# Layer-norm statistics straight from PSUM, shared work and a new instruction order in a fused gated-attention and MLP kernel

## The chip, the cores and the metric

The kernel runs on one core of one Trainium2 chip. The metric is the device time of one execution in microseconds (us).

## The reference

A gated linear attention with complex decay, then a layer norm with a two-layer MLP and a residual. B = 4 batches, H = 8 heads, S = 768 tokens, D = 48 per head, model width H x D = 384, hidden width 1536, all float32 at the outside.

```python
mag = np.sqrt(a_re * a_re + a_im * a_im)
scale = np.minimum(mag, 0.999) / (mag + 1e-06)
a_re_n, a_im_n = (a_re * scale, a_im * scale)
for t in range(S):                                   # state S_re + i S_im: D x D per head
    ar, ai = a_re_n[:, :, t, :, None], a_im_n[:, :, t, :, None]
    new_re = ar * S_re - ai * S_im
    new_im = ar * S_im + ai * S_re
    S_re, S_im = (new_re + np.einsum('bhd,bhe->bhde', k[:, :, t], v[:, :, t]), new_im)
    y[:, :, t] = np.einsum('bhd,bhde->bhe', q[:, :, t], S_re)
x = y.transpose(0, 2, 1, 3).reshape(B, S, H * D)
mu, var = mean(x), mean((x - mu) ** 2)
xn = (x - mu) / np.sqrt(var + 1e-06) * g_ln
out = x + np.maximum(xn @ w_ch1, 0.0) @ w_ch2
```

## The kernel before

The tokens are cut into 24 chunks of 128 (n = 0 to 23), worked in 12 pairs P of two chunks (`R = 2`); a batch is three pairs. Pair 0 does its front half in two parts of four heads (`PARTS`). For each pair:

- **Decay and phase.** `are`, `aim` are loaded; ScalarE (ACT) takes logs and exponentials (`ln`, `iv`, `u`), VectorE (DVE) or GpSimd the ratio `r`, its square `r2`, the log magnitude `l` and its clip `lc`. TensorE (PE) sums logs over tokens (`dec`) and angles (`ph`), ACT makes `e` and `en` (growth for queries, decay for keys), then `sin` and `cos` (`trig`). ACT's tables for logs and for trigonometry are switched by `tab`. In the pairs of `QUARTER` the cosine comes from a quarter turn added by PE (`qt`), in the others from an absolute value (`abs`).
- **Keys and queries.** `ke = k * en`, `qe = q * e`; `ks` and `qs` hold the product with the cosine (operation `.0`) and with the sine (`.1`) side by side. They are transposed by PE (`kT`, `qT`, copied to `ksT`, `qsT`) or, where the plan says S, by a DMA of the SP queue.
- **Attention.** `am` scores, `atm` masks them (DVE, or `ac` on ACT and a select on GpSimd), `y` sums values and the state `G` into a PSUM bank; `gm`, `G` carry the state, `dps` and `decc` its decay.
- **Norm.** `x` copies y from PSUM to SBUF as bf16, `bn` takes mean and variance of x, `xc` subtracts the mean, `xtr` transposes on PE and `xT` copies back. `rstd` is applied only at the end, to the MLP's output, as the ReLU lets it through.
- **MLP.** `ws` multiplies the 9 pieces of w_ch1 by g once. `mm1.P.g.part` (6 matmuls of 256 columns each) fills a group of four hidden tiles, `relu.P.g` writes them to `h`, `mm2.n.g` (4 matmuls of 384 columns) adds the group to the output bank. `ot` is `rstd * o + x`, in one DVE operation, or as `oa` on ACT and an addition on GpSimd; `st` stores it.

The weights are loaded by GpSimd's queue: `wl.0` to `wl.2` for w_ch1, `wl.3` to `wl.5` for w_ch2; all other loads, stores and DMA transposes stand in the SP queue.

Nothing is scheduled by a compiler. The order of all instructions is written out in the string `PLAN`: each token names an operation, its engine (P, A, V, G or S) and, behind it, the PSUM bank (8 in all); `@name` makes an operation of GpSimd or DVE wait for another one, so that they take turns at a port that they share. Each engine works its tokens strictly in this order. Tiles come from rings (`RINGS`), so a load waits until the tile of three pairs ago is read. `warm` operations are matmuls on constants that fill PE's waits at the start; 25 stand in the plan.

Of the kernel before, what the change touches and what calls it, by code (L numbers as in the profile page):

```python
# [41 lines left out]
qrow:G mask:G aim.1.0:S r.0.1:V one:G are.2.0:S pick:G@r.0.1 r2.0.1:A aim.2.0:S iv.0.0:A r.0.0:V r2.0.0:V
gln:S u.0.1:A ln.1.0:A k.0.1:S are.3.0:S l.0.1:V q.1.1:S lc.0.1:V u.0.0:A k.0.0:S warm.0:P0 warm.1:P0
warm.2:P0 warm.3:P0 warm.4:P0 warm.5:P0 warm.6:P0 warm.7:P0 warm.8:P0 dec.0.1:P6 l.0.0:V iv.1.0:A lc.0.0:V
zdec:V ln.2.0:A e.0.1:A6 iv.2.0:A r.1.0:V r2.1.0:V u.1.0:A r.2.0:V warm.9:P0 dec.0.0:P7 e.0.0:A7 l.1.0:V
en.0.0:A7 lc.1.0:V warm.10:P0 warm.11:P0 warm.12:P0 warm.13:P0 warm.14:P0 warm.15:P0 warm.16:P0 dec.1.0:P0
# [5 lines left out]
cos.0.1:A4 car.1.0:A2 ks.0.1.1:V ks.0.0.1:V qe.0.1.0:V qs.0.0.1:V ks.0.0.0:V ks.0.1.0:V qs.0.1.1:V qs.0.1.0:V
qs.0.0.0:V sin.1.0:A2 kT.0:P4 kT.1:P0 vf.1.0:S qT.0:P1 ksT.0:V4 ksT.1:V0 qt.1.0:P2 wl.2:G qT.1:P4 qsT.0:V1
warm.22:P5 am.0:P0 aim.3.0:S tab.log.2:A en.2.0:A6 e.2.0:A6 qsT.1:V4 v.0:G@qs.0.0.0 gm.0:P5 am.1:P6 ks.1.0.1:G
qe.1.0.0:G atm.0:V0 iv.3.0:A qs.1.0.1:G tab.trig.3:A cos.1.0:A2 q.2.0:S warm.23:P4 ph.2.0:P0 G.0:A5 y.0:P4
x.0:A4 atm.1:V6 warm.24:P6 y.1:P2 ws.1.0:V qs.1.0.0:V are.4.0:S ws.1.2:V ws.0.0:V sin.2.0:A0 bn.0:V gm.1:P5
x.1:A2 G.1:V5 ks.1.0.0:G@ws.0.0 bn.1:V xc.0:V qT.3:P4 qsT.3:A4 qt.2.0:P0 qT.2:P2 ws.0.1:V ws.0.2:A xc.1:V
kT.3:P6 cos.2.0:A0 aim.4.0:S v.1:G@xc.1 kT.2:P7 ksT.3:V6 xtr.1:P3 qsT.2:A2 xtr.0:P3 am.3:P0 ws.2.0:A xT.0:V3
ws.1.1:A ksT.2:V7 gm.2:P6 mm1.0.0.0:P4 q.3.0:S r.3.0:G am.2:P2 mm1.0.0.1:P4 qe.2.0.0:G atm.3:V0 atm.2:V2
q.2.1:S G.2:A6 y.3:P0 th.3.0:A r2.3.0:G gm.3:P6 ph.3.0:P2 x.3:A0 relu.0.0:V4 bn.3:V y.2:P7 tab.log.4:A  # L60
ln.4.0:A x.2:A7 mm1.0.1.1:P0 u.3.0:A k.2.0:S mm1.0.1.0:P0 ws.2.1:V wl.3:G ws.2.2:V mm1.0.2.0:P4 wl.4:G
# [5 lines left out]
en.3.0:A2 mm2.0.1:P6 mm2.1.1:P7 kT.4:P0 vf.2.1:S l.4.0:V lc.4.0:V kT.5:P5 rstd.0:G dec.4.0:P2 k.3.0:S
qe.3.0.1:G@lc.4.0 qsT.5:V1 ksT.4:A0 mm2.1.2:P7 ksT.5:V5 are.5.0:S k.3.1:S mm2.0.2:P6 am.4:P4 ot.1:V7
qe.3.0.0:G qs.3.0.0:V ph.4.0:P0 qs.3.0.1:V e.4.0:A2 qT.7:P7 en.4.0:A2 atm.4:V4 ke.3.0.0:G@qs.3.0.1 am.5:P2
v.2:A are.6.0:S aim.5.0:S ot.0:V6 ke.3.0.1:G car.4.0:A0 ln.5.0:A iv.5.0:A mm2.3.0:P4 y.4:P6 aim.6.0:S x.4:A6  # L70
qsT.7:V7 k.4.1:S mm2.2.0:P5 ks.3.0.0:V vf.3.1:S ln.6.0:A gm.4:P7 vf.3.0:S mm2.2.1:P5 qT.6:P6 G.4:A7 q.4.0:S
ks.3.0.1:V rstd.1:G atm.5:V2 q.4.1:S abs.4.0:A0 kT.6:P7 bn.4:V y.5:P2 mm2.2.2:P5 k.4.0:S r.5.0:G q.5.0:S
qsT.6:V6 k.5.0:S mm2.3.1:P4 ksT.6:V7 kT.7:P3 ot.2:V5 ksT.7:V3 iv.6.0:A am.6:P6 x.5:A2 mm2.3.2:P4 tab.trig.7:A
th.5.0:A r.6.0:G ac.6:A6 vf.4.0:S bn.5:V ph.5.0:P2 v.3:G xc.4:V xtr.4:P5 xc.5:V xtr.5:P5 k.6.0:S sin.4.0:A0
atm.6:G@xc.5 am.7:P6 qe.4.0.1:G st.1:S dps.3:P0 sin.5.0:A2 abs.5.0:A2 ke.4.0.0:G ot.3:V4 xT.4:V5 gm.6:P1
mm1.2.1.0:P4 decc.3:V0 G.6:A1 st.0:S vf.4.1:S are.7.0:S y.6:P0 x.6:A0 atm.7:V6 mm1.2.1.1:P4 ke.4.0.1:G gm.7:P1
qe.4.0.0:G bn.6:V y.7:P0 x.7:V0 bn.7:V mm1.2.2.0:P6 rstd.2:G xc.6:V r2.5.0:A relu.2.1:A4 aim.7.0:S
mm1.2.2.1:P6 xc.7:V cos.5.0:A th.6.0:A ks.4.0.1:V mm1.2.0.0:P4 xtr.6:P2 xtr.7:P2 are.8.0:S are.9.0:S xT.6:V2
dps.4:P0 decc.4:V0 G.7:V1 mm1.2.0.1:P4 mm1.3.2.1:P2 vf.5.0:S r2.6.0:G@ks.4.0.1 mm1.3.2.0:P2 mm1.3.0.0:P0
cos.4.0:A relu.2.0:V4 ks.4.0.0:G relu.2.2:V6 tab.log.8:A u.6.0:A v.4:V u.5.0:A l.5.0:V k.5.1:S mm1.3.0.1:P0  # L80
relu.3.0:A0 mm2.5.0:P4 mm1.3.1.1:P6 mm2.4.0:P5 qs.4.0.1:V relu.3.2:A2 qs.4.0.0:V ln.7.0:A iv.7.0:A mm2.5.1:P4
kT.9:P2 lc.5.0:V rstd.3:G dec.5.0:P0 en.5.0:A0 l.6.0:V lc.6.0:V ln.8.0:A mm2.4.1:P5 e.5.0:A0 qT.8:P3 ksT.9:V2
mm1.3.1.0:P6 ksT.8:S r.7.0:G@lc.6.0 mm2.4.2:P5 qsT.8:V3 dec.6.0:P2 ke.5.0.1:G qsT.9:S am.8:P0 iv.8.0:A
relu.3.1:V6 ke.5.0.0:V st.2:S ks.5.0.1:V ks.5.0.0:G@ks.5.0.1 gm.8:P6 mm2.5.2:P4 e.6.0:A2 en.6.0:A2 r2.7.0:A
u.7.0:A q.6.0:S atm.8:V0 mm2.6.0:P7 am.9:P2 vf.6.0:S G.8:A6 ot.5:V4 ph.6.0:P0 y.8:P4 car.6.0:A0 mm2.6.1:P7
gm.9:P6 x.8:A4 q.5.1:S tab.trig.9:A th.7.0:A q.6.1:S q.7.1:S atm.9:V2 qe.5.0.0:G y.9:P4 mm2.6.2:P7 ot.4:V5
bn.8:V mm2.7.0:P5 x.9:V4 kT.11:P4 vf.5.1:S qe.5.0.1:G abs.6.0:A0 qs.5.0.1:G bn.9:V l.7.0:V qs.5.0.0:V k.6.1:S
ph.7.0:P2 sin.6.0:A0 mm2.7.1:P5 qT.10:P0 st.3:S oa.6:A7 ksT.10:S xc.8:V xtr.8:P7 xc.9:V lc.7.0:V G.9:V6
aim.8.0:S car.7.0:A2 ke.6.0.1:G@lc.7.0 sin.7.0:A2 ke.6.0.0:G aim.10.0:S are.10.0:S xtr.9:P7 xT.8:V7 qT.11:P1
ksT.11:V4 mm2.7.2:P5 abs.7.0:A2 mm1.4.2.1:P2 qe.6.0.0:G ot.6:G mm1.4.2.0:P2 cos.6.0:A qsT.10:V0 qe.6.0.1:G  # L90
k.7.0:S tab.log.10:A ln.9.0:A qsT.11:V1 mm1.4.0.0:P6 st.4:S dps.6:P4 mm1.4.0.1:P6 v.5:G dec.7.0:P0 relu.4.2:V2
mm1.4.1.0:P2 decc.6:V4 rstd.4:G mm1.4.1.1:P2 qs.6.0.1:V relu.4.0:A6 mm2.8.0:P4 aim.9.0:S en.7.0:A0 qs.6.0.0:V
e.7.0:A0 am.11:P6 gm.10:P0 relu.4.1:A2 k.7.1:S ks.6.0.1:V q.7.0:S q.8.0:S mm2.9.0:P1 iv.9.0:A am.10:P2 r.8.0:V
mm2.8.1:P4 mm2.9.1:P1 atm.11:V6 G.10:V0 y.11:P0 atm.10:V2 vf.6.1:S qe.7.0.1:G@r.8.0 ks.6.0.0:G r.9.0:G y.10:P2
q.9.1:S ot.7:V5 mm2.9.2:P1 tab.trig.11:A cos.7.0:A th.8.0:A ph.8.0:P6 x.11:V0 kT.12:P5 x.10:A2 mm2.8.2:P4
bn.11:V bn.10:V v.6:G xc.11:V xtr.11:P0 th.9.0:A xc.10:V xtr.10:P0 qsT.12:S ot.9:V1 abs.8.0:A6
# [694 lines left out]
```

## Time and profile before

| | |
|---|---|
| runs (3) | 186.75, 186.89, 187.06 us; median 186.89 |
| profiled execution | 187.27 us, its span 185.6 us, granted clock 1.00 |
| busy | PE 173.0, ACT 160.4, DVE 153.7, GpSimd 103.6 us |
| moved by DMA | 37.29 MB, mean 201 GB/s |
| first matmul, last matmul's end | 2.2 us, 181.4 us |

The span is what the profile covers of an execution; the 1.67 us around it (187.27 - 185.6) are start and end. Busy times of engines overlap and don't add up to the span. PE is TensorE's matmuls, PEld its weight loads, DVE VectorE, ACT ScalarE, POOL GpSimd, SP the queue that issues most DMAs; L12 is line 12 of the kernel.

### The profile page before, as it was taken

How to read it: one execution, taken by the hardware profiler on the slowest of the kernel's cores; microseconds unless marked ns; L12 is line 12 of the kernel's file. 1: busy time of each engine (PE TensorE's matmuls, PEld its weight loads, DVE VectorE, ACT ScalarE, POOL GpSimd, SP SyncE). 2: the span in 40 equal slices, each digit the busy share in tenths (PEclk: the TensorE clock that was granted, in tenths of full speed). 3: DMA queues.
4: the chain of work that ended last, by engine and by line, in shares of the span. 5: the costliest groups of instructions: out<-in, count | busy, mean ns of one | idle time of the engine just before them, and what ended most of it. 6: DMA issues, size and time to landing. Idle time of an engine off the chain costs nothing.

```text
span 185.6 us, 4962 instructions
## 1 busy us (share of the span) xinstructions
PE 173.0 (93%) x1950; PEld 134.8 (73%) x1950; DVE 153.7 (83%) x298; ACT 160.4 (86%) x218; POOL 103.6 (56%) x120
## 2 busy tenths in 40 slices
PE   5887898899999999999999999999998999999990
PEld 4765576778677798777787787878776779787760
DVE  2578899999989889999889999999979987767222
ACT  5789999999999999999999999989999898536460
POOL 8203757877479699377779733374454528360110
PEclk9999999999999999999999999999999999999999
DMA  5999999899998999999999999999999999993222
GB/s 142 291 254 209 184 209 234 208 201 193 246 277 172 215 252 288 150 197 224 232 276 199 198 228 188 221 220 214 171 225 160 197 150 262 178 202 113 91 78 87
DMA packets 131879, 37.29 MB, mean 201 GB/s; under 512 B 126096, under 2 KB 131856, under 8 KB 131856
## 3 DMA queue, kind: packets, MB, share of 16 engines
q1 hardware_dynamic: 129072, 34.62, 90.0%
q0 software_dynamic: 2784, 2.36, 8.2%
q8 instruction: 15, 0.25, 0.5%
q14 instruction: 8, 0.07, 0.1%
HBM read 28.31 MB, written 4.72 MB: 178 GB/s over the span
## 4 chain that ended last, share of the span: by engine, by line
PE 74%; ACT 12%; DMA 5%; DVE 4%; issue 1%; SPq 1%; POOL 1%; POOLq 0%; ACTq 0%; DVEq 0%
PE banks L724 24%; PE banks L703 23%; PE banks L597 6%; DMA are<-in_a_re_dram 5%; PE banks L574 4%; PE banks L457 3%; ACT L759 3%; PE banks L476 2%; PE banks L647 2%; PE banks L675 2%; PE banks L650 2%; PE banks L625 2%; ACT w L428 1%; ACT th L465 1%; PE banks L472 1%
## 5 line engine op out<-in xcount | busy, mean ns | idle before, releaser
L724 PE MATMUL banks<-w2b,h 128*128 128x384 bf16 x288 | 54.9, 326 | 0.0
L703 PE MATMUL banks<-xT,w1b 128*128 128x256 bf16 x432 | 52.2, 272 | 0.2 <-DVE ksT L284 0.2
L703 PEld LDWEIGHTS <-w1b 128*128 128x128 bf16 x432 | 41.0, 98 | 6.2 <-issue 0.6
L724 PEld LDWEIGHTS <-h 128*128 128x128 bf16 x288 | 26.0, 97 | 13.3 <-ACT h L714 0.2
L714 ACT ACTIVATE h<-banks 128x1024 bf16<-128x1024 f32 x26 | 26.2, 1023 | 9.2 <-PE banks L703 9.2
L287 DVE TENSOR_TENSOR atm<-banks,mask 128x1024 bf16<-128x1024 f32 x22 | 26.7, 1220 | 5.1 <-PE banks L597 4.7
L287 POOL TENSOR_TENSOR ke<-k,en 128x384 bf16<-128x384 f32 x19 | 17.1, 914 | 19.7 <-ACT sh L511 4.2
L759 ACT ACT_TABLE_LOAD x19 | 24.4, 1283 | 1.1 <-PEq L775 0.8
L287 POOL TENSOR_TENSOR ks<-ke,trig 128x768 bf16<-128x768 bf16 x8 | 13.1, 1639 | 7.0 <-DVE qs L287 2.6
L753 PE MATMUL banks<-u_e 128*128 128x256 f32 x50 | 14.5, 430 | 2.2 <-POOL u_e L316 2.2
L736 POOL TENSOR_TENSOR ot<-ot,x 128x384 f32<-128x384 f32 x8 | 7.3, 913 | 15.3 <-DVE xc L667 8.4
L597 PE MATMUL banks<-qsT,ksT 128*128 128x128 bf16 x192 | 14.6, 219 | 1.0 <-ACT trig L517 0.7
L287 POOL TENSOR_TENSOR qe<-q,e 128x384 bf16<-128x384 f32 x14 | 12.7, 910 | 3.5 <-DVE ks L287 1.5
L597 PEld LDWEIGHTS <-ksT 128*128 128x128 bf16 x192 | 12.1, 98 | 3.3 <-DMA ksT<-ks 1.0
L660 DVE BATCH_NORM_STATS2 stats<-x 128x6 f32<-128x384 bf16 x24 | 13.3, 554 | 1.5 <-ACT x L282 1.0
L716 DVE TENSOR_SCALAR h<-banks 128x1024 bf16<-128x1024 f32 x10 | 12.1, 1218 | 2.5 <-PE banks L703 2.5
L738 DVE SCALAR_TENSOR_TENSOR ot<-banks,rstd,x 128x384 f32<-128x384 f32 x16 | 9.7, 611 | 5.4 <-PE banks L724 5.4
L428 ACT ACTIVATE w<-are 128x768 f32<-128x768 f32 (+1 forms) x13 | 10.3, 794 | 3.8 <-DMA are<-in_a_re_dram 3.5
L287 POOL TENSOR_TENSOR r<-aim,are 128x768 f16<-128x768 f32 x6 | 10.9, 1818 | 4.6 <-DVE l L449 2.9
L753 PEld LDWEIGHTS banks<-u_e 128*128 128x128 f32 x50 | 10.1, 216 | 3.6 <-POOL u_e L316 2.2
L476 PE MATMUL banks<-th,u_th 128*128 128x384 f16 (+1 forms) x52 | 11.8, 313 | 0.7 <-ACT th L465 0.7
L647 PE MATMUL banks<-v,atm 128*128 128x48 bf16 x192 | 12.2, 183 | 0.1
(93 smaller groups left out, 384.2 us busy)
## 6 DMA issues: line engine op xcount, KB each, us to landing
k<-in_k_dram SPq DMA_DIRECT2D x24, 192.0 KB, 3.8
q<-in_q_dram SPq DMA_DIRECT2D x24, 192.0 KB, 3.9
vf<-in_v_dram SPq DMA_DIRECT2D x24, 192.0 KB, 4.2
out_dram<-ot SPq DMA_DIRECT2D x24, 192.0 KB, 2.2
are<-in_a_re_dram SPq DMA_DIRECT2D x11, 384.0 KB, 5.2
aim<-in_a_im_dram SPq DMA_DIRECT2D x11, 384.0 KB, 5.3
w1b<-in_moe_w_ch_dram POOLq DMA_DIRECT2D x3, 384.0 KB, 8.0
w2b<-in_moe_w_ch_dram POOLq DMA_DIRECT2D x3, 384.0 KB, 6.3
```

The lines of the kernel that those rows point to most:

```text
L287: {"DVE": nc.vector, "POOL": nc.gpsimd}[eng(name)].tensor_tensor(**kw)
L428: add(f"ln.{X}", lambda S_=S_: act(out=S_("w"), in_=S_("are"), func=AF.Ln), needs=[f"are.{X}"], uses=[("are", P), ("w", P)])
L476: nc.tensor.matmul(heads(ps[:, c]), lhsT=u_th[:, c, j], rhs=step(T("th", P), j), start=False, stop=(j == R - 1), skip_group_check=True)
L597: nc.tensor.matmul(ps[:, h], lhsT=T("ksT", n)[:, h], rhs=T("qsT", n)[:, h], start=True, stop=True)
L647: nc.tensor.matmul(ps[:, h], lhsT=T("atm", n)[:, h], rhs=T("v", P)[:, c, h], start=True, stop=nfirst)
L660: nc.vector.bn_stats(out=T("stats", n), in_=T("x", n))
L703: nc.tensor.matmul(ps[:, jj], lhsT=w1b[:, dc, ts(gi * JG + jj, C)], rhs=T("xT", P)[:, dc].rearrange("p c t -> p (c t)"), start=(dc == 0), ...
L714: act(out=dst, in_=src, func=AF.Relu)
L716: nc.vector.tensor_scalar(out=dst, in0=src, scalar1=0.0, scalar2=None, op0=ALU.max)
L724: nc.tensor.matmul(bank(f"o.{n}")[:, 0:DM], lhsT=T("h", P)[:, j, ts(c, C)], rhs=w2b[:, j], start=(j == 0), stop=(j == NJ - 1))
L753: g.add(f"warm.{i}", lambda i=i: nc.tensor.matmul(bank(f"warm.{i}")[:, 0:256], lhsT=u_e[:, 0].rearrange("p j t -> p (j t)").bitcast(FP32), ...
L759: g.add(f"tab.{nm}.{i}", lambda tab=tab: nc.scalar.preload_act_table_set(tab))
```

## The change

- **Statistics.** `bn` reads y in PSUM. `x` is then written once, as mean minus y (bf16), by ACT (`scale=-1`, `bias=mean`) or DVE; `xc` and its tile are gone, and `xtr` transposes `x`. The sign is taken out by g, which is negated once (`gn`, on GpSimd).
- **Output.** `oa` gives `o * rstd + mean` (9 on ACT, 13 on DVE), `ot` subtracts `x` (19 on GpSimd, 3 on DVE). In the last two chunks `xr` rebuilds y from x beforehand, and the fused DVE operation follows.
- **Keys and queries.** In 16 of the 22 cases of pairs 1 to 11 one operation (`ks.P.0.2`, `qs.P.0.2`, on DVE) makes both products, the source being read twice by a step of 0. GpSimd has 7 of the single ones instead of 13.
- **GpSimd** makes 2 of the 9 weight products (`ws`), ACT 6 (3 before), DVE 1 (6 before). It makes 6 of the 13 log clips.
- **Tail.** The last ReLU of pair 11 is done in two halves (DVE and ACT), and the last chunk's second layer, output and store in two halves of 192 columns, each half in a bank of its own.
- **Order.** `PLAN` is new from end to end, engines, banks and DMA queue included. `QUARTER` is {0, 1, 2, 4} instead of {0, 1, 2, 3}. There are 25 `warm` operations as before, placed otherwise. 29 tokens have an `@` (38 before).

```diff
+    g.add("gn", lambda: nc.gpsimd.tensor_scalar(out=gln, in0=gln, scalar1=-1.0, scalar2=None,
+                                                op0=ALU.mult), needs=["gln"])
...
+                elif eng(f"ws.{jb}.{ec}") == "POOL":
+                    nc.gpsimd.tensor_tensor(out=piece, in0=piece, in1=gln[:, ds(ec, 1)].to_broadcast(
+                        [C, 512]), op=ALU.mult)
...
+                if NS == 1:
+                    def f_both(nm=nm, src=src, X=X):
+                        tt(f"{nm}.{X}.2",
+                           out=T(nm, P).rearrange("p c h (a x) -> p (c h) a x", a=2)[:, :, :, 0:D],
+                           in0=T(src, P).rearrange("p c (h d) -> p (c h) d", d=D).unsqueeze(
+                               2).to_broadcast([C, R * H, 2, D]),
+                           in1=T("trig", P).rearrange("p a c (h d) -> p (c h) a d", d=D), op=ALU.mult)
...
-            add(f"x.{n}", lambda n=n: put(f"x.{n}", T("x", n), bank(f"y.{n}")[:, 0:DM]),
-                needs=[f"y.{n}"], uses=[("x", n)], ps=(f"y.{n}", 1))
             def f_bn(n, c):
-                nc.vector.bn_stats(out=T("stats", n), in_=T("x", n))
+                nc.vector.bn_stats(out=T("stats", n), in_=bank(f"y.{n}")[:, 0:DM])
                 nc.vector.bn_aggr(out=T("mv", P)[:, c], in_=T("stats", n))
...
-                {"DVE": nc.vector, "POOL": nc.gpsimd}[eng(f"xc.{n}")].tensor_scalar(
-                    out=T("xc", n), in0=T("x", n), scalar1=mean, scalar2=None, op0=ALU.subtract)
+            def f_x(n, c):
+                mean, y = T("mv", P)[:, c, 0:1], bank(f"y.{n}")[:, 0:DM]
+                if eng(f"x.{n}") == "ACT":
+                    act(out=T("x", n), in_=y, func=AF.Identity, scale=-1.0, bias=mean)
+                else:
+                    nc.vector.tensor_scalar(out=T("x", n), in0=y, scalar1=mean, scalar2=-1.0,
+                                            op0=ALU.subtract, op1=ALU.mult)
...
+            if n < NP * R - 2:
+                def f_oa(n, c):
+                    o, scale, mean = bank(f"o.{n}")[:, 0:DM], T("rstd", P)[:, ds(c, 1)], T("mv", P)[:, c, 0:1]
+                    if eng(f"oa.{n}") == "ACT":
+                        act(out=T("ot", n), in_=o, func=AF.Identity, scale=scale, bias=mean)
+                    else:
+                        nc.vector.tensor_scalar(out=T("ot", n), in0=o, scalar1=scale, scalar2=mean,
+                                                op0=ALU.mult, op1=ALU.add)
+                add(f"ot.{n}", lambda n=n: tt(f"ot.{n}", out=T("ot", n), in0=T("ot", n), in1=T("x", n),
+                                              op=ALU.subtract),
+                    needs=[f"oa.{n}"], uses=[("x", n), ("ot", n)])
+            else:
...
+                for half, cols in enumerate(widths):
+                    tag = f".{half}" if last else ""
+                    add(f"ot.{n}{tag}", lambda n=n, c=c, cols=cols, o_of=o_of: nc.vector.scalar_tensor_tensor(
+                        out=T("ot", n)[:, cols], in0=o_of(n, cols), scalar=T("rstd", P)[:, ds(c, 1)],
+                        in1=T("ot", n)[:, cols], op0=ALU.mult, op1=ALU.add),
```

Where the steps below speak of places in the order, these are the new plan's tokens. PE's at the end of the opening, and GpSimd's around the second matrix (`ks.1.0.0` to `wl.5`):

```
PE:     ... am.2 xtr.1 gm.2 am.3 mm1.0.0.0 mm1.0.0.1 y.2 mm1.0.1.1 gm.3 y.3 ph.3.0 mm1.0.1.0 xtr.2 xtr.3
        mm1.0.2.1 mm1.0.2.0 mm1.1.1.1 mm1.1.0.0 mm1.1.1.0 mm1.1.0.1 mm1.1.2.0 mm1.1.2.1 qT.4 mm2.0.0 mm2.1.0
        qT.5 kT.4 mm2.1.1 mm2.0.1 dec.3.0 kT.5 am.4 gm.4 mm2.1.2 ...
GpSimd: ... ks.1.0.0 v.1 ws.1.0 r.3.0 ke.2.0.0 r2.3.0 wl.3 ws.2.2 qe.2.0.1 qe.2.0.0 ke.2.0.1 wl.4 r.4.0 wl.5 ...
```

Before, GpSimd's are `... ks.1.0.0 v.1 r.3.0 qe.2.0.0 r2.3.0 wl.3 wl.4 ke.2.0.0 r.4.0 wl.5 ...`.

More of the change, by code (lines that the diff above doesn't have):

```diff
@@ L42 @@
[L42 to L46, printed above, removed]
@@ L52 @@
[L52 to L56, printed above, removed]
@@ L57 @@
[L57 to L61, printed above, removed]
@@ L67 @@
[L67 to L71, printed above, removed]
@@ L72 @@
[L72 to L96, printed above, removed]
@@ new lines, in o_of, with f_mm2 @@
+            def o_of(n, cols, last=last):
+                if last:
+                    return bank2(f"o.{n}")[:, cols.start * 2 // DM, 0:DM // 2]
+                return bank(f"o.{n}")[:, cols]
+            def f_mm2(n, c, js, widths, o_of):
+                for cols in widths:
+                    for j in js:
+                        nc.tensor.matmul(o_of(n, cols), lhsT=T("h", P)[:, j, ts(c, C)],
+                                         rhs=w2b[:, j, cols], start=(j == 0), stop=(j == NJ - 1))
@@ new lines, in pair_ops @@
+            relus = [[f"relu.{P}.{part}"] for part in range(NG)]
+            if P == NP - 1:
+                relus[-1] = [f"relu.{P}.{NG - 1}.{half}" for half in range(2)]
+            for part in range(NG):
+                js, these, after = range(part * JG, part * JG + JG), widths, relus[part] + [f"wl.{NG + part}"]
+                if last and part:
+                    js, these = range(JG, NJ), widths[part - 1:part]
+                    after = relus[1] + relus[2] + [f"wl.{NG + 1}", f"wl.{NG + 2}"]
+                add(f"mm2.{n}.{part}", lambda n=n, c=c, js=js, these=these, o_of=o_of: f_mm2(n, c, js, these, o_of),
+                    needs=after + ([f"mm2.{n}.{part - 1}"] if part else []),
+                    uses=[("h", P)], ps=(f"o.{n}", len(widths)))
```

251 lines of the change are left out of this document (147 added, 104 removed), and 2 rows, old and new, of the table RINGS.

## The prediction

> **What bounds the kernel now.** I read the header of the page first, then the busy time of each engine in three stretches, then the chain of waits in order of time, then the groups of instructions by form.
>
> ```profile
> span 185.6 us, 4962 instructions
> PE 173.0 (93%) x1950; PEld 134.8 (73%) x1950; DVE 153.7 (83%) x298; ACT 160.4 (86%) x218; POOL 103.6 (56%) x120
> ```
>
> ```profile
> 0.00:42.20 42.20, 34.77 (x348) 27.46 (x349) 33.93 (x76) 37.42 (x58) 23.21 (x38) 1.00 1.02 214
> 42.20:181.40 139.20, 138.24 (x1606) 107.36 (x1602) 119.18 (x222) 122.93 (x162) 80.43 (x83) 1.00 1.00 200
> ...
> 181.40:185.60 4.20, 0.00 (x0) 0.00 (x0) 0.63 (x2) 0.00 (x0) 0.00 (x0) 1.00 0.27 96
> ```
>
> In the three rows of stretches the columns are the stretch, its length, then busy time of PE, PEld, DVE, ACT and POOL, the granted clock, the DMA share and GB/s. The page says that PE is busy 93% of the span; the stretches say where the rest lies. From 42.2 to 181.4 us PE is busy 138.24 of 139.20 us: it stands still for 0.96 us only. Before 42.2 it loses 42.20 - 34.77 = 7.4 us, and some of what counts as busy there is filling (the warm matmuls, below). After 181.4 us there are 4.2 us without any matmul. So a change that leaves PE's work alone can win at most 1 us in the long middle, something in the opening, and a part of the last 4.2 us.
>
> ```profile
> 17.02 1.28 ACT L759
> ...
> 35.56 0.66 PE banks L703 x6
> ...
> 49.41 0.89 PE banks L574 x16
> ...
> 173.54 3.27 PE banks L703 x30
> ...
> 178.77 2.61 PE banks L724 x16
> 181.41 0.62 DVE ot L738
> ```
>
> The chain (start, length, engine and line) is ACT's up to the first MLP matmuls, then PE with hardly a break, and DVE's last output (L738) at the end. PE's own pace is read here: 30 first-layer matmuls in 3.27 us are 0.109 us each, 16 second-layer ones in 2.61 us are 0.163 each, 16 transposes (L574) in 0.89 us are 0.056 each.
>
> **The costs of single operations** (mean ns is the last number before the second bar):
>
> ```profile
> L753 PE MATMUL banks<-u_e 128*128 128x256 f32 x50 | 14.5, 430 | 2.2 <-POOL u_e L316 2.2
> L660 DVE BATCH_NORM_STATS2 stats<-x 128x6 f32<-128x384 bf16 x24 | 13.3, 554 | 1.5 <-ACT x L282 1.0
> L667 DVE TENSOR_SCALAR xc<-x,mv 128x384 bf16<-128x384 bf16 x24 | 6.9, 311 | 0.3
> L284 DVE CAST x<-banks 128x384 bf16<-128x384 f32 x6 | 3.2, 538 | 0.5 <-PE banks L650 0.4
> L282 ACT CAST x<-banks 128x384 bf16<-128x384 f32 x18 | 8.7, 481 | 2.1 <-PE banks L650 2.0
> L738 DVE SCALAR_TENSOR_TENSOR ot<-banks,rstd,x 128x384 f32<-128x384 f32 x16 | 9.7, 611 | 5.4 <-PE banks L724 5.4
> L729 ACT ACTIVATE ot<-banks,rstd 128x384 f32<-128x384 f32 x8 | 4.7, 581 | 0.0
> L661 DVE BATCH_NORM_AGGREGATE mv<-stats 128x2 f32<-128x6 f32 x24 | 4.4, 182 | 0.8
> L287 DVE TENSOR_TENSOR qs<-qe,trig 128x768 bf16<-128x768 bf16 x17 | 9.2, 557 | 0.1
> L287 DVE TENSOR_TENSOR qs<-qe,trig 128x384 bf16<-128x384 bf16 x4 | 1.2, 350 | 0.0
> L287 DVE TENSOR_TENSOR r<-aim,are 128x768 f16<-128x768 f32 x5 | 4.8, 951 | 1.4 <-ACT are L430 1.4
> L449 DVE TENSOR_SCALAR l<-l 128x768 f16<-128x768 f16 x11 | 3.9, 354 | 0.2
> L368 DVE TENSOR_SCALAR w1b<-w1b,gln 128x512 bf16<-128x512 bf16 x6 | 3.2, 562 | 0.0
> L366 ACT ACTIVATE w1b<-w1b,gln 128x512 bf16<-128x512 bf16 x3 | 2.1, 730 | 0.0
> L287 POOL TENSOR_TENSOR ks<-ke,trig 128x768 bf16<-128x768 bf16 x8 | 13.1, 1639 | 7.0 <-DVE qs L287 2.6 <-PE banks L597 1.3 <-DVE w1b L368 1.3
> L736 POOL TENSOR_TENSOR ot<-ot,x 128x384 f32<-128x384 f32 x8 | 7.3, 913 | 15.3 <-DVE xc L667 8.4 <-ACT ot L729 3.9 <-DVE qs L287 2.2
> L394 POOL TENSOR_SCALAR v<-vf 128x768 bf16<-128x768 f32 x6 | 5.0, 830 | 6.3 <-DMA vf<-in_v_dram 5.5 <-DVE xc L667 0.8
> ```
>
> **PE's work stays.** Both orders hold 25 warm matmuls (the x50 of L753 are two passes each). One queries' transpose goes and one keys' comes; the last chunk's 12 second-layer matmuls become 24 of half width, the same columns. So nothing comes off PE, and the sum is made of waits.
>
> **Statistics and centring, 24 chunks.** Before: copy (ACT 0.481 or DVE 0.538), statistics 0.554 and 0.182, centring 0.311; chain 0.48 + 0.55 + 0.18 + 0.31 = 1.52 us, hand-offs apart. After: statistics from PSUM, then one centred copy. Statistics from PSUM have no row: below, the SBUF row 0.554; above, the heaviest PSUM row of this width, 0.611. I take 0.56, as the plain cast from PSUM (0.538) is no slower than statistics from SBUF. The centred copy lies between 0.481 and 0.581 on ACT and at 0.54 on DVE. Chain: 0.56 + 0.18 + 0.54 = 1.28 us, 0.24 us shorter; but the PSUM bank is held for all of it, not for 0.48. Counting PE's planned work between a chunk's y and the next use of that bank, the median is 2.0 us before and 3.2 after, with 0.8 us as the shortest outside the middle (chunk 0, where x is late in both), so the order pays for it. In DVE time: the 24 centrings go (-7.5), 8 more copies come (+4.3).
>
> The Trainium skill ("VectorE: DVE Perf Modes", Rules for kernel authors) speaks against this: it says to copy PSUM to SBUF first when a matmul output is read often, as PSUM reads get no fast mode. The rows show that here: 0.311 from SBUF against 0.538 from PSUM. But a copy with two SBUF readers is 0.54 + 0.55 + 0.31 = 1.40 and two PSUM readers are 0.56 + 0.54 = 1.10, so with two readers the copy doesn't pay; by the rule the sum would be 0.3 us a chunk worse, on an engine that doesn't set the end.
>
> **Output.** DVE's 16 fused outputs (0.611) become 13 scalings on DVE (0.54 to 0.58), 9 on ACT (0.581, one more) and 22 subtractions, 19 of them on GpSimd (0.913): DVE -9.7 + 7.3 + 3 x 0.6 and the tail's three, about +0.8; GpSimd +10.0. All of it lies behind the last use of the chunk and is hidden by PE.
>
> **Keys and queries.** 16 products of twice the width replace 32: width costs (0.557 - 0.350) / 384 = 0.54 ns an element, so 0.557 + 768 x 0.54 / 1000 = 0.97 us against 1.11 for two on DVE or 3.28 on GpSimd. The start alone is then 0.350 - 384 x 0.54 / 1000 = 0.14. The other bound is the rate of the f32 products, (0.951 - 0.14) / 768 = 1.05 ns an element: 0.14 + 1536 x 1.05 / 1000 = 1.75 us. I take 0.97, since type, place and inner runs are those of the 0.557 row. GpSimd loses 6 products (-9.8), DVE gains about 1.
>
> **Log clips and weights.** Six clips go to GpSimd (DVE 0.354 each; there, nearest the 0.830 row, 0.4 to 1.5 each). Two weight pieces go there too, between 0.913 and 1.639, say 1.16; three more on ACT (0.730). DVE drops 5 (0.35 to 0.56). The new sign flip of g (under 0.2 us on GpSimd) has its data 10 us early and hides.
>
> Sum by engine: DVE about -8, ACT about -2 (8 copies, one table load and one query copy less; weights, one and a half relus and others more), GpSimd about +14. None of the three exceeds PE's share after that: 146, 158 and 118 us.
>
> **The opening.** Laid out by hand from the rows with the new order: ACT has the same operations up to its table load at 17.02 us and the same ones from there to the first chunk's copy, so keys, queries and phases come at the same times. After it ACT has three more weight pieces (+2.2) and one relu, and two copies and one query copy less (-2.0); DVE has the opposite. The first MLP matmul comes at about 35.9 instead of 35.56, and the closed stretch begins at 42.4 instead of 42.3. I put 0, with 0.9 us either way for what a layout by hand misses.
>
> **The middle.** Nearly all of the 0.96 us stands in two rows of the timeline, whose brackets give the idle time before:
>
> ```profile
> 91.30 0.93 PE L703 MATMUL banks<-xT,w1b 128*128 128x256 bf16 x7 [0.23 <-DVE ksT L284]
> 143.25 0.62 PE L597 MATMUL banks<-qsT,ksT 128*128 128x128 bf16 x8 [0.71 <-ACT trig L517]
> ```
>
> The first waits for a copy on DVE, the second for scores' operands (pair 9). With a shorter chain to xT and 8 us less on DVE I credit half of 0.96: -0.5. Ends: -1.0 and, for the new order's own waits, the first rival.
>
> **The tail.** After the last matmul stand L738 at full width, then a store. Half width: 0.611 - 192 x 1.05 / 1000 = 0.41, so -0.2; the last matmul is half as wide, -0.08; the last store carries half the bytes.
>
> ```profile
> out_dram<-ot SPq DMA_DIRECT2D x2, 192.0 KB, 1.9
> ```
>
> Of its 1.9 us to landing most is fixed; I put -0.07. Tail: -0.35, ends -0.1 and -0.5. The extra store issue is hidden by 8 half matmuls (0.65 us).
>
> **Sum.** -0.35 - 0.5 + 0 = -0.85. The profiled execution took 187.27 us for its span of 185.6; the median of the three runs is 186.89, so 0.38 lower. Profiled: span 184.75; against the median 186.89 - 0.85 = 186.0 us.
>
> **Rivals.** What a measurement of this kernel tells from no change is taken as 0.2%, 0.37 us.
>
> (1) The second matrix comes late; slower. Its three loads (wl.3 to wl.5) are issued by GpSimd; the last row, of the page, has their median from issue to landing.
>
> ```profile
> 38.79 1.59 POOL L357 DMA_DIRECT2D w2b<-in_moe_w_ch_dram  x2
> 45.73 0.81 POOL L357 DMA_DIRECT2D w2b<-in_moe_w_ch_dram  x1
> ...
> w2b<-in_moe_w_ch_dram POOLq DMA_DIRECT2D x3, 384.0 KB, 6.3
> ```
>
> Before, two go at 38.79 and the third at 45.73. In the new order one weight piece and three decays stand between the first and the second: 1.16 + 3 x 0.91 = 3.9 us. By hand the second goes out at 43.1 and the third, behind a ratio that waits for DVE's new product, at 46.5. With 6.3 us they land at 49.4 and 52.8. The order wants them at about 50.0 (at 42.4 there are 7.5 groups of first-layer matmuls left, 4.9 us; then two groups of the second, 1.3, and 24 transposes, 1.35) and, after 3.2 us more of decays, transposes, scores and second layer, at 53.2. It decides at 0.5 us: if landings take over 7 us, PE, whose queue holds the tail of the second layer and everything behind it, stands still for 1 to 1.5 us and nothing wins that back. 186.0 + 1.5 = 187.5. For it: no reserve. Against it: the 6.3 is a median. Chance 0.20.
>
> (2) The wide product runs at the f32 rate: 16 x (1.75 - 0.97) = 12.5 us more on DVE. In the middle DVE (119 of 139) could hold it, but pairs 2 and 3 have four of them within 42 to 57 us, where keys are awaited: 4 x 0.78 less some cover, +2.5, 188.5. It decides at 1.2 us a product. Chance 0.10.
>
> (3) PE's clock falls in the opening. The new order has one warm matmul after the phases of pair 0 where the old has four. Path work of about 3 us from the transposes to the first layer would run at half pace: +1.5 or more, 187.5. The granted clock is 1.00 in the first stretch too, where PE is busy 34.77 of 42.20 us. The Trainium skill ("TensorE: Matmul & The Clock Gate", What's actually happening) lets the clock fall after an idle window of about 3.4 us; by hand no gap here is over 1 us. Chance 0.05.
>
> (4) Nothing but the tail: the waits of the middle move elsewhere, as an order that is packed as tightly has as many. -0.35: 186.5, about at the bound. Chance 0.15.
>
> My forecast has the other 0.50. Faster 0.50, same 0.15, slower 0.20 + 0.10 + 0.05 = 0.35. Range: the low end takes the far ends of middle, tail and opening, 186.9 - 1.0 - 0.5 - 0.9 = 184.5; the high end takes in rivals 1 and 2: 188.6.
>
> **What would show it.** After: the wide products at 0.97; statistics from PSUM at 0.55 to 0.61; PE idle under 1 us from 42 to the last matmul; the last output of DVE at 0.41; the loads of w2b landed before 50 and 53. Wrong would be: a PE gap over 0.5 us in the middle (rival 1 if the weight load ends it, 2 if a DVE product does), or first-layer matmuls that begin a microsecond or more away from 35.9.

## The result, and the profile after

The changed kernel takes 193.95 us (median of 6 runs, 193.44 to 195.09); the kernel before, run beside it, 187.02. The ratio is 1.0368, with a 95% interval of 1.0329 to 1.0408: 3.7% slower, where I forecast 0.5% faster. The profiled execution took 193.73 us, its span 192.0 (before 187.27 and 185.6). Ratios, here and below, leave out runs that took over 1.5% longer than the fastest run of their kernel.

The header of the page after, its busy times, and the two stretches up to the last matmul's end (same columns as in the prediction):

```profile
span 192.0 us, 4968 instructions
PE 174.9 (91%) x1962; PEld 136.4 (71%) x1962; DVE 150.1 (78%) x263; ACT 161.8 (84%) x214; POOL 130.1 (68%) x138
```

```profile
0.00:42.20 42.20, 33.35 (x331) 26.66 (x332) 30.41 (x66) 36.44 (x56) 28.68 (x40) 1.00 1.01 213
42.20:188.50 146.30, 141.51 (x1634) 109.75 (x1631) 119.30 (x197) 125.41 (x159) 101.42 (x99) 1.00 0.96 191
```

No engine became the bound. The last matmul ends 7.1 us later than before (188.5 for 181.4). From 42.2 us on PE stands still for 146.30 - 141.51 = 4.8 us where it had 0.96, which is 3.8 us of it. In the opening it stands still for 42.20 - 33.35 = 8.85 us instead of 7.4, another 1.4; the first MLP matmul starts at 38.0 us, before at 35.4. The remaining 1.9 us are a longer busy time of PE (174.9 for 173.0), which I have not taken apart. What PE waits for over the whole span, in the view of waits (total, times, longest):

```profile
PE banks L459 <- POOL l L451: 4.1, 4, 1.6
...
PE banks L586 <- DVE qs L283: 2.2, 2, 1.8
PE banks L609 <- DMA vf<-in_v_dram: 0.9, 1, 0.9
...
PE banks L750 <- DMA w2b<-in_moe_w_ch_dram: 0.6, 1, 0.6
PE banks L474 <- DVE atm L283: 0.6, 1, 0.6
```

In the first row the decays (L459) wait for the log clip (L451) on GpSimd. Two of these four waits stand in the opening, where PE waited for VectorE's clips before, too (1.7 us then, 2.0 now). New are the two in the middle, 0.53 and 1.52 us; they are 2.05 of its 4.8 us, and the rows of vf, w2b and atm (0.9, 0.6, 0.6) are most of the rest. The groups by form say why a clip is waited for. The mean ns of one is the last number before the second bar:

```profile
L451 POOL TENSOR_SCALAR l<-l 128x768 f16<-128x768 f16 x5 | 13.9, 2783 | 9.1 <-DVE l L448 7.6 <-DVE qe L283 1.4
L451 POOL TENSOR_SCALAR l<-l 128x384 f16<-128x384 f16 x1 | 1.7, 1706 | 0.1
L451 DVE TENSOR_SCALAR l<-l 128x768 f16<-128x768 f16 x6 | 2.2, 365 | 0.1
```

A clip takes 2.78 us on GpSimd, 7.6 times what it takes on DVE, and almost twice the upper end of my range (0.4 to 1.5). One of them in the timeline, with the decay that waits for it (start, length, idle time before in brackets):

```profile
117.09 2.79 POOL L451 TENSOR_SCALAR l<-l 128x768 f16<-128x768 f16 x1 [0.99 <-DVE l L448]
...
119.93 0.81 PE L459 MATMUL banks<-l,u_e 128*128 128x384 f16 x4 [1.52 <-POOL l L451]
```

PE can do nothing behind `dec.8.0` in its order until the clip ends. What else GpSimd holds in its own order behind a clip comes late too: in the opening that is the load of w_ch1, told below.

### The profile page after: what moved, and what is told of

Same layout as the page of the kernel before. It is cut to its first block, busy times and chain, and to the rows that moved or that the text cites. A ratio compares the mean times of both kernels' runs of the same rounds, so it can differ in the third digit from the quotient of the medians.

```text
span 192.0 us, 4968 instructions
## 1 busy us (share of the span) xinstructions
PE 174.9 (91%) x1962; PEld 136.4 (71%) x1962; DVE 150.1 (78%) x263; ACT 161.8 (84%) x214; POOL 130.1 (68%) x138
## 4 chain that ended last, share of the span: by engine, by line
PE 49%; DVE 14%; POOL 11%; DMA 11%; SPq 6%; issue 5%; ACT 3%; POOLq 0%; DVEq 0%; ACTq 0%
PE banks L750 16%; PE banks L715 15%; DMA w1b<-in_moe_w_ch_dram 4%; SPq L386 4%; POOL l L451 4%; PE banks L609 3%; PE banks L586 3%; DVE atm L283 2%; DMA aim<-in_a_im_dram 2%; PE banks L459 2%; DMA vf<-in_v_dram 2%; PE banks L478 2%; DMA k<-in_k_dram 2%; DVE h L733 2%; POOL qe L283 2%
## 5 line engine op out<-in xcount | busy, mean ns | idle before, releaser
L750 PE MATMUL banks<-w2b,h 128*128 128x384 bf16 (+1 forms) x300 | 55.5, 319 | 0.8 <-DMA w2b<-in_moe_w_ch_dram 0.6
L731 ACT ACTIVATE h<-banks 128x1024 bf16<-128x1024 f32 (+1 forms) x28 | 27.9, 1005 | 7.6 <-PE banks L715 7.6
L451 POOL TENSOR_SCALAR l<-l 128x768 f16<-128x768 f16 (+1 forms) x6 | 15.6, 2604 | 9.1 <-DVE l L448 7.6
L283 POOL TENSOR_TENSOR ot<-ot,x 128x384 f32<-128x384 f32 x19 | 17.1, 914 | 5.9 <-DVE ot L769 2.5
L283 POOL TENSOR_TENSOR qe<-q,e 128x384 bf16<-128x384 f32 x17 | 15.6, 929 | 6.2 <-DVE car L286 5.1
L283 DVE TENSOR_TENSOR ks<-ke,trig 128x1536 bf16<-128x1536 bf16 (+2 forms) x14 | 10.7, 773 | 6.3 <-POOL ke L283 6.3
L669 DVE BATCH_NORM_STATS2 stats<-banks 128x6 f32<-128x384 f32 x24 | 13.4, 557 | 2.0 <-ACT h L731 0.8
L459 PE MATMUL banks<-l,u_e 128*128 128x384 f16 (+1 forms) x52 | 9.9, 313 | 4.1 <-POOL l L451 4.1
L448 DVE SCALAR_TENSOR_TENSOR l<-r,w 128x768 f16<-128x768 f16 (+1 forms) x13 | 12.1, 929 | 1.9 <-ACT r L444 1.8
L283 DVE TENSOR_TENSOR qs<-qe,trig 128x1536 bf16<-128x1536 bf16 (+2 forms) x15 | 11.1, 750 | 2.0 <-issue 1.5
L733 DVE TENSOR_SCALAR h<-banks 128x1024 bf16<-128x1024 f32 (+1 forms) x9 | 10.4, 1157 | 2.6 <-PE banks L715 2.6
## 6 DMA issues: line engine op xcount, KB each, us to landing
q<-in_q_dram SPq DMA_DIRECT2D x24, 192.0 KB, 4.1
k<-in_k_dram SPq DMA_DIRECT2D x24, 192.0 KB, 4.0
vf<-in_v_dram SPq DMA_DIRECT2D x24, 192.0 KB, 3.9
out_dram<-ot SPq DMA_DIRECT2D x23, 192.0 KB, 2.3
```

The source lines that it names most:

```text
L283: {"DVE": nc.vector, "POOL": nc.gpsimd}[eng(name)].tensor_tensor(**kw)
L448: nc.vector.scalar_tensor_tensor(out=S_("l"), in0=S_("r2"), scalar=0.5, in1=S_("w"), op0=ALU.mult, op1=ALU.add)
L451: add(f"lc.{X}", lambda X=X, S_=S_: {"DVE": nc.vector, "POOL": nc.gpsimd}[eng(f"lc.{X}")].tensor_scalar(out=S_("l"), in0=S_("l"), scalar1= ...
L459: nc.tensor.matmul(heads(ps[:, c]), lhsT=u_e[:, c, j], rhs=step(T("l", P), j), start=(j == 0), stop=(j == R - 1))
L669: nc.vector.bn_stats(out=T("stats", n), in_=bank(f"y.{n}")[:, 0:DM])
L731: act(out=dst, in_=src, func=AF.Relu)
```

## The experiments

They stand in the order of the argument; what an expectation calls the first experiment is number 4 here. The kernel before ran again beside each group of them, with medians of 188.69 us (experiments 1 to 4), 187.31 (5 to 8), 187.68 (9, 10 and 12) and 187.51 (11). Since these alone differ by over 1 us, times of different groups are compared by their ratio to before, and the lengths of two single profiles of different groups can't be told apart to a microsecond.

**1. Clips on GpSimd without the minimum.** The kernel after; the same six places, size and type. It leaves out the upper clip of these pieces.

```diff
-                out=S_("l"), in0=S_("l"), scalar1=LNCAP, scalar2=LNEPS, op0=ALU.min, op1=ALU.add),
+                out=S_("l"), in0=S_("l"), scalar1=1.0 if eng(f"lc.{X}") == "POOL" else LNCAP, scalar2=LNEPS, op0=ALU.mult if eng(f"lc.{X}") == "POOL" else ALU.min, op1=ALU.add),
```

> The kernel after, its six log clips of GpSimd with mult by 1.0 in place of the min (the upper clip of these six pieces is left out; type, size, place and the addition stay). If the min is what makes the operation dear: each about 0.8 to 1.0 us at 768 columns and a time within 1 us of the run with the clips on VectorE. If float16, the operation in place or two steps are dear: 2.78 us each and a time of 193.5 to 194.5 us.

Measured: 189.65 us (10 runs), ratio to before 1.0007 (0.9956 to 1.0059). Groups, and the stretch from 42.2 us to the last matmul:

```profile
L451 POOL TENSOR_SCALAR l<-l 128x768 f16<-128x768 f16 x5 | 4.2, 832 | 9.0 <-DVE l L448 5.2 <-PE banks L586 2.3 <-DVE qe L283 1.4
```

```profile
42.20:183.60 141.40, 140.91 (x1636) 109.87 (x1633) 119.13 (x199) 125.08 (x159) 92.29 (x98) 1.00 0.97 197
```

It is the minimum that is dear. With a multiplication in its place the operation takes the 0.83 us of the row that I had priced it by, the ratio falls from 1.0368 to 1.0007, and PE's idle time of the middle falls from 4.8 to 141.40 - 140.91 = 0.49 us. The waits for vf and atm go with it and the one for w2b falls to 0.2 us, though the edit touches none of them.

**2. Which forms are dear.** The kernel before, with seven operations more on GpSimd behind its last output.

> The kernel before with seven probes on GpSimd behind its last output, each in place on a tile that is no longer used: min and add on 768 columns of float16, on 384 of float16, mult and add on 768 of float16, min alone on 768 of float16, min and add on 768 of bfloat16, min and add and then mult and add on 768 of float32. If the min is dear: the first, second, fourth, fifth and sixth at about 2.8, 1.7, 2.8, 2.8, 2.8 us and the mult ones at 0.8 to 1.0. If float16 is dear: the first four at 2.8, 1.7, 2.8, 2.8 us and the last two at 0.8 to 1.0. If two steps are dear: only the fourth is near 0.8. If the size of a tile in place is all that counts, all but the second are alike.

Five of the seven in the timeline (min and add on 768 float16; on 384; min alone; min and add on bfloat16; on float32), and mult and add on float32:

```profile
176.07 2.80 POOL L766 TENSOR_SCALAR r<-r 128x768 f16<-128x768 f16 x1
178.96 1.50 POOL L766 TENSOR_SCALAR r<-r 128x384 f16<-128x384 f16 x1
...
181.45 2.13 POOL L766 TENSOR_SCALAR r<-r 128x768 f16<-128x768 f16 x1
183.65 2.78 POOL L766 TENSOR_SCALAR ke<-ke 128x768 bf16<-128x768 bf16 x1
186.49 2.77 POOL L766 TENSOR_SCALAR are<-are 128x768 f32<-128x768 f32 x1
...
189.34 0.83 POOL L766 TENSOR_SCALAR are<-are 128x768 f32<-128x768 f32 x1
```

The seventh, mult and add on float16, took 0.83 us too. Neither the type nor having two steps decides: a minimum with an addition costs 2.8 us in each of the three types, a multiplication with an addition 0.83 in the two that were tried, and a minimum alone (float16) 2.13. Between 384 and 768 columns it is (2.80 - 1.50) / 384 = 3.4 ns a column. The minimum alone, 0.67 us cheaper than with the addition, fits none of my four cases exactly: I had put it at 2.8 or at 0.8.

**3. This part of the change alone, on the kernel before.** The six tokens `lc.*:V` become `lc.*:G`.

> The kernel before, with the same six log clips on GpSimd, at the same places of its order: this part of the change alone. Theory 1: 2.78 us each at 768 columns, and 2 to 6 us slower than before, 189 to 193 us. Theory 2: within 1 us of before, 186.5 to 188.

Measured: 196.7 us (4 runs), ratio 1.0386 (1.0267 to 1.0505), more than I expected. Its clips and PE's first wait:

```profile
L449 POOL TENSOR_SCALAR l<-l 128x768 f16<-128x768 f16 x5 | 14.6, 2916 | 8.2 <-DVE l L446 4.3 <-PE banks L457 3.0 <-DMA k<-in_k_dram 0.9
```

```profile
PE banks L457 <- POOL l L449: 5.3, 4, 2.3
```

So the clips alone cost as much as the whole change did: experiment 1 takes the part away, experiment 3 does it alone, and each moves the time by 3.6 to 3.9%. They don't do it at the same places. In experiment 3 the opening is as before (first MLP matmul at 35.7 us) and PE stands still for 6.95 us from 42.2 us on; in the kernel after it is 4.8 us there, and a part of the loss lies in the opening. That the two sizes agree so closely is partly chance.

**4. Clips back on VectorE, at the places that they have in the new order.** The tokens alone; what stands between them is left out.

```diff
-lc.0.1:G ... lc.2.0:G@qe.0.0.0 ... lc.3.0:G@l.3.0 ... lc.6.0:G@l.6.0 ... lc.7.0:G ... lc.8.0:G@l.8.0
+lc.0.1:V ... lc.2.0:V ... lc.3.0:V ... lc.6.0:V ... lc.7.0:V ... lc.8.0:V
```

> The kernel after, with its six log clips of GpSimd (lc.0.1, 2.0, 3.0, 6.0, 7.0, 8.0) put back on VectorE at the same places in the order. Theory 1 (the clip costs 2.78 us on GpSimd in place of about 0.83, and the decays, keys and loads behind it come late): GpSimd's busy time falls by about 16 us to 114, VectorE's rises by 2 us, PE's idle time from 42 to 188 us falls from 4.75 to under 2, and the time is 186.5 to 188.5 us. Theory 2 (the new order or the statistics from PSUM are slow by themselves): 191 us or more. Theory 3 (part of it is the angles' load of the first pair, moved behind another in SP's queue, 6.4 us of waiting in place of 4.6): 188.5 to 191, with the loss left in the opening.

Four runs from 190.04 to 195.37 us, at a granted clock of 0.982 to 0.991: too scattered for a ratio, and above the 186.5 to 188.5 that I expected. GpSimd's busy time fell to 112.6 us, as expected. The profile is of the longest run (195.37 us), so what it shows of the opening isn't shown for the shortest:

```profile
30.62 0.90 POOL L283 TENSOR_TENSOR ke<-k,en 128x384 bf16<-128x384 f32 x1 [7.84 <-DMA k<-in_k_dram]
```

```profile
36.27 0.99 PE L586 MATMUL banks<-ident,qs 128*128 128x128 bf16 x10 [3.98 <-POOL qs L283]
```

Without the clip in front of it, GpSimd issued the first load of w_ch1 at 16.6 us instead of 21.3, ahead of the key load `k.1.1` (19.2). The keys landed at 30.5 us instead of 24.3, GpSimd waited 7.84 us for them, and PE 3.98 us for the queries that follow on GpSimd; the first MLP matmul came at 42.3 us. In this run an engine set free started a transfer that took another's place.

**5. The same with the weight load held.** `wl.0:G` becomes `wl.0:G@ke.0.0.0`.

> The first experiment's kernel (clips on VectorE at the clips' old places) with one wait more: the first load of w_ch1 waits for ke.0.0.0 and so is issued near 19 us, not at 16.6. If the loss of the first experiment in the opening came from that load overtaking k.1.1: k.1.1 lands near 26 us instead of 30.5, PE's stop of 4.1 us at 32 us falls to under 1.5, and the time is 3 us below that run, 187 to 189.5. Else 190 or more.

Measured: 189.48 us (4 runs, 188.84 to 190.15), ratio 1.0114 (1.0057 to 1.0171). `k.1.1` landed at 25.1 us, and PE's longest wait for the queries was 0.7 us: as expected. The first MLP matmul came at 37.2 us. How much time the hold wins is open, as experiment 4's shortest run (190.04) is no further from before than these. What is left in the middle has a place of its own, the clip of pair 8, which on VectorE stands behind the statistics of two chunks:

```profile
115.28 0.82 PE L459 MATMUL banks<-l,u_e 128*128 128x384 f16 x4 [1.19 <-DVE l L451]
```

**6. Early key load alone, on the kernel after.** `k.1.1:S` goes right behind `k.1.0:S`.

> The kernel after with one edit: k.1.1 right behind k.1.0 in SP's queue. The clips stay on GpSimd. If the late key sets GpSimd's chain to pair 1's queries: 1 to 2 us faster than the kernel after, 192 to 193. If the dear clip in front of it (18.5 to 21.2 us) hides that: 193.5 to 194.5.

Measured: 193.69 us (4 runs), ratio 1.0342 (1.0267 to 1.0418), not to be told from the kernel after. But the runs fall into two pairs, 192.44 and 192.56 us at a granted clock of 1.000, 194.82 and 195.25 at 0.991; the first pair lies where I expected it if the late key counted. The profile is of the longest run. VectorE in it:

```profile
32.34 0.35 DVE L370 TENSOR_SCALAR w1b<-w1b,gln 128x512 bf16<-128x512 bf16 x1 [2.37 <-DMA w1b<-in_moe_w_ch_dram]
```

In this run the dear clip hides the key's gain (the first MLP matmul comes at 39.7 us), through a chain that I hadn't seen: GpSimd issues the loads of w_ch1 behind the clip (18.0 to 20.8 us here), VectorE's weight piece `ws.1.1` waits for the second of them, and pair 1's product `qs.1.0.0` stands behind that piece.

**7. All three: clips on VectorE, each right behind its log; early key load; weight load held.**

> The kernel after with three edits: its six log clips of GpSimd on VectorE, each right behind its log; the load of pair 1's second half of keys (k.1.1) right behind k.1.0 in SP's queue instead of eight loads later; the first load of w_ch1 held until ke.0.0.0, so that the free GpSimd doesn't bring it forward. Theory 1 with the key's load as the cause of what was left in the opening: k.1.1 lands before 20 us, PE's wait at 31 us for pair 1's queries goes, first MLP matmul at 36 or before, and 185.5 to 187 us. If the rest of the new order is slower by itself (or the statistics from PSUM): 188 or more.

Measured: 186.85 us (12 runs), ratio 0.9993 (0.9958 to 1.0028); the profiled span is 184.6 us. The first MLP matmul starts at 35.4 us, as before. VectorE at the same piece, and the middle:

```profile
29.70 0.35 DVE L370 TENSOR_SCALAR w1b<-w1b,gln 128x512 bf16<-128x512 bf16 x1 [0.32 <-issue]
```

```profile
42.20:181.20 139.00, 138.35 (x1609) 107.62 (x1607) 118.65 (x197) 122.39 (x156) 86.84 (x92) 1.00 0.99 201
```

In the profiles of experiments 5 and 6 either repair alone leaves the opening late (37.2 and 39.7 us), and both together bring it back. The clips stand at earlier places here than in experiment 5, so the early key isn't the only difference.

**8. The first pair's angles earlier as well.** `aim.0.1:S` goes right behind `are.0.1:S`.

> As the kernel before it in this list, and the first pair's angles (aim.0.1) are loaded second in SP's queue, as in the kernel before, not third. If the ratio's wait for them (6.4 us against 4.6) sets the first decay: 0.5 to 1 us faster. If warm matmuls and later waits cover it: no change.

Measured: 187.31 us (12 runs), ratio 1.0001 (0.9971 to 1.0031): no change from experiment 7, the second case of the expectation.

**9. Copy before square.** In experiment 7's kernel `r2.4.0:V` goes behind `qsT.4:V5`.

> The kernel of clips on VectorE, early key load and held weight load, with one edit more: VectorE copies pair 2's queries (qsT.4) before it squares the ratio of pair 4 (r2.4.0), not after. Expected: PE's stop of 0.70 us at 48.3 us, where pair 2's key transpose waits for that copy, goes, and the profiled span is 0.5 to 0.7 us below that kernel's 184.6. If the key product itself (1.62 us there) is what comes last: no change.

Measured: 187.16 us (12 runs), ratio 0.9976 (0.9947 to 1.0004); the span of its profile is 184.1, 0.5 us less, and PE's stop at 48.3 us is gone. The ratio's interval holds 1, so the time doesn't show a gain.

**10. Values wait for the key product.** In that kernel `v.2:G` becomes `v.2:G@ks.2.0.2`.

> The kernel with the copy before the square, and GpSimd's v.2 waits for VectorE's product ks.2.0.2. If the two slow each other (1.59 and 1.62 us side by side, against 0.83 and 0.95 alone): both come back to about 0.83 and 0.95 and up to 0.5 us is won near 48 us. If not: ks.2.0.2 stays at 1.5 or more.

Measured: 186.93 us against 187.68 beside it (12 and 28 runs), ratio 0.9956 (0.9922 to 0.9991): the only version here that is faster than before by more than its interval, and by little; it can't be told from experiment 9. The pair in experiment 9, then here:

```profile
45.93 1.61 DVE L283 TENSOR_TENSOR ks<-ke,trig 128x1536 bf16<-128x1536 bf16 x1
...
46.65 1.58 POOL L396 TENSOR_SCALAR v<-vf 128x768 bf16<-128x768 f32 x1
```

```profile
46.16 0.95 DVE L283 TENSOR_TENSOR ks<-ke,trig 128x1536 bf16<-128x1536 bf16 x1
...
47.20 0.82 POOL L396 TENSOR_SCALAR v<-vf 128x768 bf16<-128x768 f32 x1 [0.37 <-DVE ks L283]
```

Both come back to what they take alone. Its profiled span (185.1 us) is no shorter than experiment 9's; there a load of w_ch2 came late, the prediction's first rival:

```profile
50.00 1.30 PE L750 MATMUL banks<-w2b,h 128*128 128x384 bf16 x7 [0.57 <-DMA w2b<-in_moe_w_ch_dram]
```

**11. The second matrix earlier.** `wl.4:G` goes right behind `wl.3:G`.

> The kernel in which v.2 waits, with the second load of w_ch2 (wl.4) issued right behind the first (wl.3), as in the kernel before, ahead of a weight piece and three decays. In the run without it the load landed at 49.95 us and the second-layer matmuls stood still for 0.73 us until then (rival 1 of the prediction). Expected: landed by 47 us, that wait gone, and 0.3 to 0.7 us faster: profiled span about 184.5 and time about 186.3. If the load, being earlier, delays other loads or GpSimd's decays: no change.

Measured: 187.17 us against 187.51 (12 and 16 runs), ratio 0.9986 (0.9944 to 1.0028). The load landed at 48.6 us instead of 49.95 and that wait is gone, but the time didn't fall: span 185.4. In this run the first MLP matmul came at 36.6 us, in experiment 10's at 35.8, and the moved load goes out only after that delay began. Inconclusive for the time; the wait itself is explained. This kernel holds all of experiment 10's edits, and its ratio's interval holds 1, so the 0.4% of experiment 10 did not show a second time.

**12. The tail alone, on the kernel before.** The last four hidden tiles, the output and the store in two halves; the last ReLU stays whole.

> The kernel before, with the tail's part of the change alone: in the last chunk the last four hidden tiles' products, the output and the store go in two halves of 192 columns, each half with a bank of its own. By the prediction's term: from the last matmul's end to the end of the span 0.27 us less than before's 4.19. By the traces of the changed kernels: 0.6 to 0.8 less. Time 186.2 to 186.9 where before has 186.9.

Measured: 187.22 us (12 runs), ratio 0.9986 (0.9949 to 1.0023); from the last matmul's end to the end of the span 4.25 us, before 4.19. Nothing is won, where I expected 0.27 or 0.6 to 0.8 us. Here only four half matmuls lie between the halves, and the last store is issued 0.27 us after its output ended (181.0, 181.27), since SP still issues the one before; in the changed kernel eight lie between, and it is 0.03 us.

## Why the prediction was wrong, point by point

**The step that failed** is the log clips: "there, nearest the 0.830 row, 0.4 to 1.5 each". The row (L394) is a one-input operation of the same form on GpSimd, but not with the same arithmetic, and the profile's lines name the form and not the arithmetic. A minimum had no row on GpSimd in the trace before, and the range should have been open at the top. Six at 0.83 would be 5.0 us; they took 13.9 + 1.7 = 15.6, and GpSimd's sum came out at 130.1, not 118. By experiment 1 this term carries the 3.7%, to within that run's interval (0.9956 to 1.0059). The sum held it at nothing on PE's path, since only busy times per engine were compared; VectorE's and ACT's came out at 150.1 and 161.8 us, not 146 and 158, and no engine passed PE in any case.

**The opening** (0, with 0.9 either way) was the second miss. The first MLP matmul came at 38.0 us, not 35.9. I wrote that keys, queries and phases come at the same times, and went through ACT's and DVE's operations, not SP's queue for `k.1.1` nor GpSimd's for the first matrix. VectorE and PE after:

```profile
32.09 0.35 DVE L370 TENSOR_SCALAR w1b<-w1b,gln 128x512 bf16<-128x512 bf16 x1 [1.64 <-DMA w1b<-in_moe_w_ch_dram]
```

```profile
33.30 0.89 PE L586 MATMUL banks<-ident,qs 128*128 128x128 bf16 x13 [1.78 <-DVE qs L283]
```

With the cheap clip, in the profile of experiment 1, the first MLP matmul still came at 38.4 us: `k.1.1` landed at 26.2, GpSimd's products of pair 1 ran beside the weight piece on VectorE (1.83 us there, 0.35 in experiment 7), and the granted clock fell (below). Experiment 7 mends both, 35.4 us. What the late opening costs in time stays open: experiment 1's profile is late by 3.0 us there, and its runs still can't be told from before's.

**The middle** (-0.5) came out in size but for the clips: 0.49 us idle in experiment 1, against 0.96, and 0.65 in experiment 7. The two waits that I had credited are gone in both, and others stand in their place; that the shorter chain did it was not tried.

**The tail** (-0.35) had the right sign and was too small. From the last matmul's end to the end of the span it is 192.02 - 188.47 = 3.55 us, against 4.19. The last output:

```profile
188.50 0.42 DVE L789 SCALAR_TENSOR_TENSOR ot<-banks,rstd,ot 128x192 f32<-128x192 f32 x1 [0.16 <-PE banks L750]
```

0.42 is what I had; the last store landed 1.62 us after its issue, not 1.86, where I had credited 0.07; the rest came after that landing and stays unexplained. Experiment 12 shows that halves alone don't bring it.

**The single terms**, from the groups after:

```profile
L669 DVE BATCH_NORM_STATS2 stats<-banks 128x6 f32<-128x384 f32 x24 | 13.4, 557 | 2.0 <-ACT h L731 0.8 <-PE banks L662 0.8
L679 DVE TENSOR_SCALAR x<-banks,mv 128x384 bf16<-128x384 f32 x14 | 8.3, 613 | 0.3
L677 ACT ACTIVATE x<-banks,mv 128x384 bf16<-128x384 f32 x10 | 5.8, 580 | 2.3 <-DVE mv L670 1.8 <-PE banks L662 0.5
L769 DVE TENSOR_SCALAR ot<-banks,rstd,mv 128x384 f32<-128x384 f32 x13 | 8.7, 671 | 1.8 <-PE banks L750 1.7 <-POOL rstd L703 0.2
L767 ACT ACTIVATE ot<-banks,mv,rstd 128x384 f32<-128x384 f32 x9 | 6.0, 670 | 0.3 <-PE banks L750 0.2
L283 DVE TENSOR_TENSOR ks<-ke,trig 128x1536 bf16<-128x1536 bf16 x8 | 7.6, 951 | 4.3 <-POOL ke L283 4.3
L367 POOL TENSOR_TENSOR w1b<-w1b,gln 128x512 bf16<-128x512 bf16 x2 | 2.1, 1046 | 0.0
```

Statistics from PSUM (0.557 for 0.56), the wide product (0.951 for 0.97) and the weight piece on GpSimd (1.05 for 1.16) were right. The centred copy on VectorE (0.61 for 0.54) and the scaling (0.67, for 0.54 to 0.58) cost more; on ACT the copy (0.58) lies at the upper end of what I gave. Both take per-token operands from SBUF, which the plain copies did not; whether that is the cause was not tried. In experiment 7, which keeps them all, PE's idle time in the middle is 0.65 us, so they cost nothing that shows.

**The rivals.** (1) The second matrix came late, as described, but for 0.6 us in the profile after, not 1.5. (2) The wide product didn't run at the f32 rate. (3) The clock was 1.00 in the profiled execution, but 0.987 to 0.991 in the other five runs of the changed kernel. Their spans, 191.7 to 193.4 us, lie on both sides of the profiled 192.0, so a fall of the clock doesn't make the 3.7%. Where it falls can be seen in the run of experiment 1, in which PE stood waiting for pair 1's queries; in experiment 7's it did not fall there:

```profile
32.38 1.60 PE L586 MATMUL banks<-ident,qs 128*128 128x128 bf16 x16 [1.26 <-DVE qs L283]
```

```profile
30.00:36.00 6.00, 3.98 (x51) 3.56 (x51) 4.71 (x7) 4.49 (x8) 5.30 (x6) 0.72 0.97 228
```

```profile
30.00:36.00 6.00, 5.53 (x95) 4.84 (x95) 5.89 (x11) 6.00 (x11) 5.41 (x5) 1.00 0.96 225
```

The rule that the prediction cites from the Trainium skill ("TensorE: Matmul & The Clock Gate", What's actually happening) wants an idle window of about 3.4 us; PE's waits at this place are 1.26 us and shorter, though PE was busy for only 0.36 of the 2 us from 30 to 32. So by this run shorter waits, close together, go with a fall; what set it off wasn't tried. (4) fell with the forecast. None of the four was the clip: I priced GpSimd's new work once, and then asked only whether its sum exceeded PE's, not which of its operations stands alone between a log on DVE and a decay on PE.

With clip and key load mended (experiment 7) the profiled span is 184.57 us; the forecast's was 184.75. That they agree is luck in part: up to the last matmul's end 0.2 us are won, behind it 0.8, where the forecast had 0.58 and 0.27. Of the time this shows little: before's runs beside it go from 186.04 to 188.95 us, and the ratio is 0.9993. So the forecast's gain stands in one profile and isn't shown by the runs; only with experiments 9 and 10 on top does a gain of 0.4% come out of its interval, and experiment 11 doesn't repeat it.

## What to carry to other kernels

Price an operation that moves to another engine by the arithmetic it does there, not by a row of the same form; if the trace has no such row, leave the range open at the top and ask who waits for this one operation. An engine that issues loads sets, by how long its operations take, when they go out: making it slower delayed one load here (21.3 us, where it went at 19.2 in experiment 1), and making it faster let that load (16.6 us in experiment 4) overtake another that was wanted sooner, so follow every queue behind a moved operation. An engine's sum below the bound says nothing of a single operation that stands alone between two others.
